# Packed attention with a gated convolution: the low-word pass of the float64 weights and eight scaled query tables move to GpSimd, with a new issue order

## The chip, the core and the metric

The kernel runs on one core of a Trainium2 chip. The metric is the device time of one execution in microseconds. The core has four compute engines with queues of their own: TensorE (PE; its weight loads are listed as PEld), VectorE (DVE), ScalarE (ACT) and GpSimd (POOL). SyncE (SP) issues all transfers here.

## The reference, cut to what matters

```python
def sm_attn(qq, kk, vv):                      # 8 batches, 8 heads, head size 64
    s = scale * np.matmul(qq, kk.transpose(0, 1, 3, 2))
    s = s - np.max(s, axis=-1, keepdims=True)
    a = np.exp(s)
    a = a / (np.sum(a, axis=-1, keepdims=True) + 1e-09)
    return np.matmul(a, vv)
p_packed = sm_attn(p, k, v)                   # 32 packed queries against 576 keys
x = sm_attn(q, p_packed, p_packed)            # 576 queries against the 32 packed rows

h = np.maximum(x @ w_in, 0.0)                 # 512 -> 1024
conv_out = sum over 3 taps of conv_w[k] * h shifted along the sequence
out = (h * sigmoid(conv_out)) @ w_out         # 1024 -> 512, 8 x 576 rows
```

q, k, v and p come as float32. w_in, conv_w and w_out come as float64, so each weight is a pair of 32-bit words and has to be narrowed on the core.

## The kernel before, in words

Sixteen head groups g (four heads of one batch each, two groups to a batch) run through the same steps. `queries(g)` (L481) makes two copies of the packed queries scaled by 1/8, the tile `pm` (ACT, L484), transposes it on PE (L487) and copies the result to `pT`. `head_transpose` (L420) brings keys and queries into the layout that PE needs: for the first four groups by PE transposes (L444) and ACT copies (L450), later by DVE (L427). `attention(g)` (L509) computes scores of keys (L460), a maximum on DVE (`nm`, L515), the exponential on ACT (`a`, L519), transposes `a` on PE (L547), multiplies by v (L557), scales to `pb` (L576), transposes that to `ppT` (L581, L584), computes the scores of the queries (L460 again), and then a softmax of six DVE passes over 128x576 (L591 to L615). The result is split in a high and a low part, `a2hi` (ACT, L619) and `a2lo` (DVE, L621).

`packed_weight(b, hf)` (L632) multiplies the packed rows of batch b with one half of w_in (PE, L641), and splits the sum in `ghi` (ACT, L656) and `glo` (for the first two batches by PE and ACT, L660 and L664). `ffn1(b, j)` (L689) then has eight steps j for a batch. One step, a unit below, is 24 matmuls of L705, a copy out of PSUM (ACT, L717), three DVE passes and two ACT passes. A unit waits for a2 and for glo of its batch. `ffn2` and what follows it (L794 and the products of L926) multiply by w_out.

The weights come as eight tiles of 128x1024 pairs, four of w_in (i = 0 to 3) and four of w_out (i = 4 to 7), into three staging areas: one tile `stage`, and two parts of a tile that the trace shows as `hgt`. `narrow` (L267) makes float32 of a tile in three passes: ACT rescales the upper words in place (L275), DVE turns the low words into a three-bit integer in place (L277), DVE joins the two (L282). The first two need only the landed tile. Tiles 0 and 1 are needed by `packed_weight(0, 0)`, tiles 2 and 3 by `packed_weight(0, 1)`.

The order of the work is written out: `ORDER` is a list of two-digit numbers of streams, `Flow.run` takes the next step of that stream each time, and each engine's queue gets its instructions in that order. `Flow` also estimates when each step can start, from costs written into the steps and from constants. The estimate has one effect on the program: where it sees PE idle before the step "second" (the first L794), `fill` places matmuls of the identity with itself, the tile `idle` (L251), in PE's queue. They compute nothing that is used.

Of the kernel before, what the change touches and what calls it, by code (L numbers as in the profile page):

```python
# [13 lines left out]
ALU = mybir.AluOpType  # L14
# [7 lines left out]
    "0002043m0408043u0304030305060b3l0c06013k050b060c0g0c0c0b060605053q3v3k0e06070e070a3k063v06063k0j060e3v09060j3s0k"  # L22
    "0f0j0o060k0e0f3n0k0i0h3r3r060k0d063k0e0m0d3k3r060d0r0e0e0d060e060e060m060e0m0r3t0m0m3t0s0r400e3w0w0s0e0s0n0z0e0e"
    "3t0s0l0e0n060z0z0l0l0e3y170e46460m0q060m0e0u0e0u0l0m460m0e41460p410m170m0e0m0u17480u3x493x480v410v0m0u3x48410m4a"
    "49484a10474849474a3z0m414948413z491f4a49124248470u0u4a4a474b124b0t490u124b0t14433z0u0t0m4a434b0m4c0t4d1f4b4b434c"
    "0u441f4d0x4c4b3z12120u4e18434e3z1a0u4c120m4d4c4g3o6e130u1a154c3z0u131a124c6e450m0u434e4d45126e0u4e434g4f0m456e4g"
    "1a0u1n0m0u124f6e1n451l4d4e4f6e0u454f4d1a4h1c4e4e0u0u4f4g1b0y1k4d451b4i4f4f114j4i881n884k4i6e1g4h6f4j6e6e4i6f6e4k"
    "4h4k4i4j4i89161i121a4k4j4i6e1i6f6f121e1a4j4k4l891d126f6f6f6f4j4k4l1i6f1o4k6g121s4l1i4l6g4h124l8a4m1a4l6f1a1j4m1q"
    "191j1i1a6f4m4j121i6g1q8a1w6g6h6e4n6g4m6h1q204n1a1v6g1i6g4m1v4l1h6g4m1a4n124m121r1v4n6g6g236f8b1a6g4o121i4n1i4o4p"
    "6h6h4o4p4p1a236h124o8b4o6h4n1q6g4p1a6h6h6h4p6h4o1m4o1a1y4n234p4p1q1i6h1i1q4q282b1y4r6i1r1y6i1y1a1i6i126i6i1q1a2b"  # L30
    "4r6i12241a4q4q1z6i6j1a6i1a4r1i6i6i4s6i2b1p4s6j4s1q4t4u1q4s1i1y1i4t4s264t1t4t1q1z6k1y2g6j2c4u6j1y4u4s261i6j2j4u6j"
    "4s6k6j264u2j4v4t2j1q6j271i4u1u4v226i4u6j266j4t2e1x4w2k6j4t1i4v1q2e1i1q6k4w2e4v2a1i1q6h2f2e4v3p6k6k6k4w1y1i274x26"
    "6k1q6k6l1y4x6l216k6k6k2f4x1q6k4x2m1y4v50266m1q6l6l4w264v1q26262r2m6l2h4w6l2m2r506l4x2r6j6l4y4w2e1q2n2z4y4y2z1y1y"
# [19 lines left out]
class Step:  # L53
# [5 lines left out]
    def __init__(self, engine, ns, after=(), take=(), give=(), sets=None, cols=0, tiled=False, parts=1, loose=False):  # L59
        self.engine, self.ns, self.after, self.take, self.give = engine, ns, after, take, give  # L60
        self.sets, self.cols, self.tiled, self.parts, self.loose = sets, cols, tiled, parts, loose


class Flow:
# [14 lines left out]
        "DVE": dict(PE=256, ACT=128, DVE=127, SP=200, POOL=200),  # L79
        "DATA": dict(PE=300, ACT=300, DVE=300, SP=0, POOL=0),  # L80
    }
    ISSUE = dict(SP=(465, 1100), POOL=(1050, 1000))
    LATER, LANES = 620, 8
    SLOW = ((4600, 1.28), (5500, 1.7))

    def __init__(self, tokens, warm, busy):
        self.tokens = {k: [(0.0, None)] * n for k, n in tokens.items()}
        self.warm, self.busy = warm, busy
        self.done = {}
        self.free = dict(PE=2500.0, ACT=1900.0, DVE=600.0, SP=580.0, POOL=1350.0)  # L90
        self.data = 2700.0
        self.issued = 0
        self.flights = [0.0] * 7
        self.windows = {}
        self.tiled = False
        self.streams = []
# [4 lines left out]
    def earliest(self, step, last):  # L101
# [3 lines left out]
        at = max([t + self.LAG[e][step.engine] if e else 0.0 for t, e in froms], default=0.0)  # L105
        return max(at, self.free[step.engine] + (self.tail(step.tiled) if step.engine == "PE" else 0))
# [36 lines left out]
    def transfers(self, step, at):  # L143
        issue, delay = self.ISSUE[step.engine]
        for _ in range(step.parts):
            if step.engine == "SP":
                at = max(at, self.flights.pop(0))
            at += self.LATER if step.engine == "SP" and self.issued >= self.LANES else issue
            self.issued += step.engine == "SP"
            slow = next((x for t, x in self.SLOW if self.data < t), 1.0)  # L150
            self.data = max(self.data, at + delay) + step.ns / step.parts * slow
            if step.engine == "SP":
                self.flights.append(self.data)
        return at, self.data

    def run(self, order):
        for n in order:
# [12 lines left out]
            elif step.engine in self.ISSUE:  # L170
                self.free[engine], t = self.transfers(step, at)
                end = (t, "DATA")
            else:
                end = (at + step.ns, engine)
                self.free[engine] = end[0]
            for name in step.give:
# [8 lines left out]
def tile_packed_attention_conv_gate(  # L185
# [11 lines left out]
    nc = tc.nc  # L197
# [19 lines left out]
    PE_LO = 2  # L217
    HALVED = 4
# [50 lines left out]
    def narrow(key, out, raw, m, after=(), take=(), sets=None):  # L269
# [30 lines left out]
    def load_weight(i):  # L300
        _, _, src, st = weight_tile(i)
        yield Step("SP", 2500, after=[("wp", i - 3)] if i >= 3 else [], sets=[("wd", i)])
# [80 lines left out]
    def load_v(g):  # L383
        b, gg = divmod(g, NG)
        yield Step("SP", 2250, take=["v"], sets=[("v", g)], parts=2)
# [683 lines left out]
```

## Time and profile before

| what | value |
|---|---|
| median of 3 runs | 402.41 us (402.21 to 402.48) |
| the profiled execution's own time | 402.01 us |
| its span | 400.2 us |
| PE busy | 392.2 us, 98% of the span |
| DVE busy | 365.5 us, 91% |
| ACT busy | 284.1 us, 71% |
| POOL busy | 1.6 us |
| bytes moved | 49.19 MB |

Times of rows are in microseconds from the start of the span. The profiled execution took 1.8 us more than its span. Busy times of PE come from modelled ends, so consecutive matmuls overlap a little in the rows; the distance from one start to the next is the better measure of what one costs.

### The profile page before, as it was taken

To read this page: it belongs to the slowest core of one execution; us is meant where nothing else is said; L and a number is where in the kernel's file an instruction comes from. 1 tells how busy PE (TensorE), PEld (TensorE's weight loads), DVE (VectorE), ACT (ScalarE), POOL (GpSimd) and SP (SyncE) were. 2 spreads that over 40 slices of the span, in tenths; PEclk is the share of its full clock that TensorE was granted. 3 is DMA by queue.
4 is the path that set the end of the run, shared out by engine and by line. 5 is a ranking of instruction groups with operands and counts; after the bars stand their busy time and mean duration, and the time that the engine had idled before them with its cause. 6 is when DMAs were issued, how large, how long until landed. Compare 5 with 4: busy or idle time off the path is not lost.

```text
span 400.2 us, 8463 instructions
## 1 busy us (share of the span) xinstructions
PE 392.2 (98%) x3393; PEld 318.8 (80%) x3393; DVE 365.5 (91%) x532; ACT 284.1 (71%) x497; POOL 1.6 (0%) x16
## 2 busy tenths in 40 slices
PE   7899999999999999999999999999999999999996
PEld 6668676778868877878869687878788787889996
DVE  0789999999999999999999999999999999999751
ACT  4989999977687588666765659738657678876440
POOL 1000000000000000000000000000000000000000
PEclk9999999999999999999999999999999999999999
DMA  8999999999858782966483539113600110001202
GB/s 304 357 361 267 276 264 163 128 156 146 121 94 112 122 196 68 156 88 153 79 153 79 97 100 157 48 51 97 122 2 27 52 41 19 23 2 52 78 28 79
DMA packets 140378, 49.19 MB, mean 123 GB/s; under 512 B 121244, under 2 KB 132788, under 8 KB 140340
## 3 DMA queue, kind: packets, MB, share of 16 engines
q1 hardware_dynamic: 140340, 48.67, 55.8%
q8 instruction: 26, 0.43, 0.5%
q14 instruction: 12, 0.10, 0.1%
HBM read 37.25 MB, written 9.44 MB: 117 GB/s over the span
## 4 chain that ended last, share of the span: by engine, by line
PE 84%; ACT 8%; DMA 5%; SPq 1%; issue 1%
PE fo L794 44%; PE big L705 23%; PE big L460 3%; PE big L641 3%; DMA q<-in_q_dram 3%; PE big L926 3%; DMA v<-in_v_dram 2%; PE sm L926 2%; PE sm L557 2%; ACT hgt L731 1%; ACT hgt L721 1%; PE big L547 1%; ACT hgt L275 1%; ACT glo L664 1%; SPq L404 1%; PE sm L794 1%
## 5 line engine op out<-in xcount | busy, mean ns | idle before, releaser
L794 PE MATMUL fo<-wo_hi,xhi 128*128 128x512 f32 x240 | 97.9, 408 | 0.0
L794 PE MATMUL fo<-wo_lo,xhi 128*128 128x512 f32 x240 | 94.8, 395 | 0.0
L794 PE MATMUL fo<-wo_hi,xlo 128*128 128x512 f32 x240 | 94.5, 394 | 0.0
L717 ACT ACTIVATE hbuf<-big 128x576 f32<-128x576 f32 x64 | 42.3, 668 | 30.1 <-PE big L705 29.5
L731 ACT ACTIVATE hgt<-hgt 128x576 f32<-128x576 f32 x64 | 43.9, 696 | 18.8 <-DVE hgt L727 18.6
L794 PEld LDWEIGHTS fo<-wo_hi,xhi 128*128 128x128 f32 x240 | 45.3, 189 | 13.3 <-issue 2.5
L705 PE MATMUL big<-a2hi,ghi 128*128 128x288 f32 x256 | 55.6, 298 | 0.1
L705 PE MATMUL big<-a2hi,glo 128*128 128x288 f32 x256 | 54.5, 294 | 0.0
L705 PE MATMUL big<-a2lo,ghi 128*128 128x288 f32 x256 | 54.3, 294 | 0.0
L794 PEld LDWEIGHTS fo<-wo_lo,xhi 128*128 128x128 f32 x240 | 45.1, 188 | 11.2
L723 DVE SCALAR_TENSOR_TENSOR hgt<-hbuf,cw,hgt 128x576 f32<-128x576 f32 x64 | 51.1, 802 | 2.5 <-ACT hgt L721 2.3
L794 PEld LDWEIGHTS fo<-wo_hi,xlo 128*128 128x128 f32 x240 | 45.1, 188 | 7.9
L727 DVE SCALAR_TENSOR_TENSOR hgt<-hbuf,cw,hgt 128x576 f32<-128x576 f32 x64 | 50.7, 803 | 0.4
L721 ACT ACTIVATE hgt<-hbuf,cw 128x576 f32<-128x576 f32 x64 | 50.3, 792 | 1.0
L733 DVE SCALAR_TENSOR_TENSOR hgt<-hgt,hbuf 128x576 f32<-128x576 f32 x64 | 47.1, 745 | 0.7 <-ACT hgt L731 0.4
L705 PEld LDWEIGHTS big<-a2hi,ghi 128*128 128x128 f32 x256 | 42.7, 188 | 5.1 <-ACT glo L664 1.0
L705 PEld LDWEIGHTS big<-a2lo,ghi 128*128 128x128 f32 x256 | 40.9, 188 | 0.0
L705 PEld LDWEIGHTS big<-a2hi,glo 128*128 128x128 f32 x256 | 40.9, 188 | 0.0
L747 DVE TENSOR_TENSOR xlo<-hgt,xhi 128x1024 fp32r<-128x1024 f32 (+1 forms) x36 | 35.8, 1002 | 0.0
L858 ACT COPY o<-fo 128x512 f32<-128x512 f32 (+1 forms) x32 | 18.5, 580 | 21.2 <-PE fo L794 19.6
L744 ACT CAST xhi<-hgt 128x1024 fp32r<-128x1024 f32 (+1 forms) x36 | 31.5, 881 | 2.2 <-DVE hgt L733 2.2
L515 DVE TENSOR_REDUCE nm<-big 128x1 f32<-128x576 f32 x16 | 11.9, 746 | 11.6 <-PE big L460 11.5
(191 smaller groups left out, 604.1 us busy)
## 6 DMA issues: line engine op xcount, KB each, us to landing
out_dram<-o SPq DMA_DIRECT2D x35, 256.0 KB, 3.3
v<-in_v_dram SPq DMA_DIRECT2D x16, 512.0 KB, 5.9
k<-in_k_dram SPq DMA_DIRECT2D x48, 144.0 KB, 4.2
q<-in_q_dram SPq DMA_DIRECT2D x48, 144.0 KB, 4.1
hgt<-in_moe_w_in_dram SPq DMA_DIRECT2D x3, 1024.0 KB, 11.2
hgt<-in_moe_w_out_dram SPq DMA_DIRECT2D x3, 1024.0 KB, 6.6
a1T<-stage SPq DMA_DIRECT2D x96, 20.0 KB, 1.8
hgt<-in_k_dram SPq DMA_DIRECT2D x2, 576.0 KB, 5.1
```

Of the source, the lines that this page charges most:

```text
L705: nc.tensor.matmul(out=t[:, hf, :SH], lhsT=w[:, gg, js], rhs=x[:, hf * SH : (hf + 1) * SH], start=n == 0, stop=n == 3 * NG - 1,)
L717: nc.scalar.activation(out=h[:, 1 : S + 1].rearrange("c (f s) -> c f s", f=2), in_=t[:, :, :SH], func=AF.Relu, scale=0.5)
L721: nc.scalar.activation(out=d, in_=h[:, 1 : S + 1], func=AF.Copy, scale=cw[:, NJ + j : NJ + j + 1])
L723: nc.vector.scalar_tensor_tensor(out=d, in0=h[:, 0:S], scalar=cw[:, j : j + 1], in1=d, op0=ALU.mult, op1=ALU.add)
L727: nc.vector.scalar_tensor_tensor(out=d, in0=h[:, 2 : S + 2], scalar=cw[:, 2 * NJ + j : 2 * NJ + j + 1], in1=d, op0=ALU.mult, op1=ALU.add)
L731: nc.scalar.activation(out=d, in_=d, func=AF.Tanh)
L733: nc.vector.scalar_tensor_tensor(out=d, in0=d, scalar=1.0, in1=h[:, 1 : S + 1], op0=ALU.add, op1=ALU.mult)
L744: nc.scalar.copy(out=hi[:, js, o], in_=src[:, js])
L747: nc.vector.tensor_tensor(out=lo[:, js, o], in0=src[:, js], in1=hi[:, js, o].bitcast(F32), op=ALU.subtract)
L794: nc.tensor.matmul(out=t[:, : fs.stop - fs.start], lhsT=x, rhs=w[:, c, fs], start=c + i == 0, stop=c == NJ - 1 and i == 2)
L858: nc.scalar.copy(out=o[:, fs], in_=sums_of[m, q][:, : fs.stop - fs.start])
L926: nc.tensor.matmul(out=turns[m, bank][:, at : at + 256], lhsT=x[:, c, :], rhs=y[:, c, :], start=first and c + i == 0, stop=c == 3 and i == ...
```

## The change

The lines of the new file that matter, without the new list of numbers (two of its lines stand for it) and without the marks `cols=1` that nine more DVE steps got:

```diff
-    "0002043m0408043u0304030305060b3l0c06013k050b060c0g0c0c0b060605053q3v3k0e06070e070a3k063v06063k0j060e3v09060j3s0k"
+    "000404040402053l3m080303030505060106050b0b3k0b060j3u070c0c0c0j0j060c0e3k07060e3k060606063k0r060e063v0g3k3k0k0k0a"
...
+        "POOL": dict(PE=300, ACT=300, DVE=300, SP=300, POOL=150),
...
-    ISSUE = dict(SP=(465, 1100), POOL=(1050, 1000))
-    LATER, LANES = 620, 8
+    ISSUE = dict(SP=(465, 1100), POOL=(900, 1000))
+    LATER, LANES = 640, 8
...
+    ROOMY, SLACK = 60000, 500
+    RING = 288
...
+        if step.engine in ("DVE", "POOL") and step.cols:
+            at = max(at, self.port)
...
+                while self.queued and (self.queued[0][0] <= at or sum(n for _, n in self.queued) + step.ring > self.RING):
+                    at = max(at, self.queued.pop(0)[0])
...
+    SCALED = 8
+    BY_POOL = range(8)
+    POOL_LOW, POOL_BOTH = 1500, 2200
...
-        yield Step("DVE", 68 + m * 100 // 192, after=after, loose=True)
-        nc.vector.tensor_scalar(
+        pool = key in BY_POOL
+        side = nc.gpsimd if pool else nc.vector
+        at = Step("POOL", POOL_LOW, after=after, loose=True, parts=0, sets=[("low", key)], cols=1)
+        yield at if pool else Step("DVE", 68 + m * 100 // 192, after=after, loose=True, cols=1)
+        side.tensor_scalar(
             out=low.bitcast(I32), in0=low.bitcast(U32), scalar1=2.0**-29, scalar2=7.0, op0=ALU.mult, op1=ALU.min
         )
-        yield Step("DVE", 69 + m * 100 // 96, after=[("up", key)], take=take, sets=sets)
+        yield Step("DVE", 69 + m * 100 // 96, after=[("up", key)] + [("low", key)] * pool, take=take, sets=sets, cols=1)
...
-        yield Step("ACT", 200, after=[("p", g // 4)] + [("pT", g - 1)] * (g > 0), take=["pm"])
+        pool = g < SCALED
+        after = [("p", g // 4)] + [("pT", g - 1)] * (g > 0)
+        yield Step("POOL", 400, after=after, take=["pm"], parts=0, cols=1) if pool else Step("ACT", 200, after=after, take=["pm"])
...
-        nc.scalar.mul(out=pm, in_=packs[g // 4][:, g % 4, :].unsqueeze(1).broadcast_to([128, 2, D]), mul=SCALE)
+        twice = packs[g // 4][:, g % 4, :].unsqueeze(1).broadcast_to([128, 2, D])
+        if pool:
+            nc.gpsimd.tensor_scalar(out=pm, in0=twice, scalar1=SCALE, scalar2=None, op0=ALU.mult)
+        else:
+            nc.scalar.mul(out=pm, in_=twice, mul=SCALE)
```

So the low-word passes of all eight weight tiles leave DVE for POOL, the small one of conv_w stays on DVE, and `pm` of groups 0 to 7 leaves ACT for POOL. In `Flow`, DVE steps that carry the mark `cols=1` and POOL's steps never overlap; transfers are held back by a limit of queued work, `RING`; and after 60 us a transfer counts as landed 0.5 us later. `Flow` itself runs on no engine: what is left of it in the program is the order and the fillers.

The order moves three places of which the prediction speaks. The new file's lines are 23 to 29 higher. The first is SP's queue, where the first weights are loaded (`stage` and `hgt_77` are staging areas; `hgt_76` holds the first keys and queries). Before:

```order
L349 DMA s_158<-in_moe_conv_w_dram 24x256
L404 DMA k<-in_k_dram 128x1152
L305 DMA hgt_77<-in_moe_w_in_dram 128x2x1024
L404 DMA hgt_76<-in_q_dram 128x1152
L388 DMA v<-in_v_dram 128x4x256
L392 DMA v<-in_v_dram 64x4x64
L305 DMA hgt_77<-in_moe_w_in_dram 128x2x1024
L404 DMA k<-in_k_dram 128x1152
L477 DMA p<-in_p_dram 128x4x64
L404 DMA q<-in_q_dram 128x1152
```

The same place now:

```order
L372 DMA s_156<-in_moe_conv_w_dram 24x256
L328 DMA stage<-in_moe_w_in_dram 128x2x1024
L427 DMA k<-in_k_dram 128x1152
L427 DMA hgt_76<-in_q_dram 128x1152
L328 DMA hgt_77<-in_moe_w_in_dram 128x2x1024
L411 DMA v<-in_v_dram 128x4x256
L415 DMA v<-in_v_dram 64x4x64
L328 DMA hgt_77<-in_moe_w_in_dram 128x2x1024
L427 DMA k<-in_k_dram 128x1152
L427 DMA q<-in_q_dram 128x1152
```

The queries of group 1 (`hgt_76`) now come ahead of weight tile 1, tile 0 (`stage`) behind the first v and conv_w, and the queries of group 2 (`q`) ahead of the second load of p.

The second is ACT's queue from `ghi` of the first packed weight to the copy-out of the first unit. Before:

```order
L656 CAST ghi<-big 128x1024
L576 ACTIVATE pb<-sm,rs 128x128
L450 COPY qT<-big 128x512
L584 COPY ppT<-sm 128x128
L619 CAST a2hi<-a2t 128x576
L275 ACTIVATE stage<-stage 128x1024
L664 CAST glo<-big 128x1024
L519 ACTIVATE a_564,sm_565<-big,nm 128x576
L493 COPY pT<-sm 128x2x32 x2
L275 ACTIVATE hgt_77<-hgt_77 128x1024
L717 ACTIVATE hbuf_78<-big 128x576
```

The same place now:

```order
L685 CAST ghi<-big 128x1024
L295 ACTIVATE stage<-stage 128x1024
L548 ACTIVATE a_494,sm_495<-big,nm 128x576
L473 COPY qT<-big 128x512
L605 ACTIVATE pb<-sm,rs 128x128
L648 CAST a2hi<-a2t 128x576
L613 COPY ppT<-sm 128x128
L693 CAST glo<-big 128x1024
L356 CAST wo_hi<-tmp 128x1024
L295 ACTIVATE hgt_77<-hgt_77 128x1024
L524 COPY pT<-sm 128x128
L746 ACTIVATE hbuf_78<-big 128x576
```

The exponential of group 3 stands ahead of `glo` now, and `wo_hi` ahead of the first copy-out.

The third is POOL's queue after its work of setting up. Before:

```order
L246 MEMSET v 64x4x64
masks.py:199 ISA
masks.py:199 AFFINE_SELECT ident<-ident 128x128
L246 MEMSET v 64x4x64
L527 MEMSET stage 128x2x32 x2
```

The same place now:

```order
L511 TENSOR_SCALAR pm<-p 128x128 x4
L300 TENSOR_SCALAR stage<-stage 128x1024
L300 TENSOR_SCALAR hgt_77<-hgt_77 128x1024 x2
L300 TENSOR_SCALAR stage<-stage 128x1024
L511 TENSOR_SCALAR pm<-p 128x128
L300 TENSOR_SCALAR hgt_77<-hgt_77 128x1024
L511 TENSOR_SCALAR pm<-p 128x128
L300 TENSOR_SCALAR hgt_77<-hgt_77 128x1024
L511 TENSOR_SCALAR pm<-p 128x128
L300 TENSOR_SCALAR hgt_77<-hgt_77 128x1024 x2
L511 TENSOR_SCALAR pm<-p 128x128
L556 MEMSET stage 128x2x32 x2
```

Sixteen instructions were added there: four tables, tiles 0, 1, 2 and 4, and then tables and tiles by turns, so that a tile can stand behind a table that has to wait.

On PE the order holds 35 filler calls before and 33 now; 31 stand ahead of the first unit in both, 4 behind it before, 2 now.

## Rows read from the trace of the kernel before

**Rows 1.** The page: share of the span and instructions of PE.
```profile
PE 392.2 (98%) x3393; PEld 318.8 (80%) x3393; DVE 365.5 (91%) x532; ACT 284.1 (71%) x497; POOL 1.6 (0%) x16
```

**Rows 2.** Windows: length; busy PE, PEld, DVE, ACT, POOL (instructions); PEclk, DMA share, GB/s.
```profile
16.00:24.00 8.00, 6.41 (x95) 5.13 (x95) 7.25 (x13) 5.61 (x13) 0.00 (x0) 1.00 1.06 362
32.00:40.00 8.00, 8.00 (x73) 7.18 (x74) 7.83 (x13) 8.00 (x15) 0.24 (x2) 1.00 1.01 232
...
80.00:140.00 60.00, 60.00 (x614) 47.90 (x614) 59.50 (x90) 42.83 (x82) 0.00 (x0) 1.00 0.86 125
```

**Rows 3.** The tile idle (fillers): ns min/median/max, first and last start.
```profile
L251 PE MATMUL idle<-ident x70: 271/275/579, 1.7 to 48.3; 128*128 128x128 f32 x70
```

**Rows 4.** PE's timeline: start, busy, line, operation, [idle before it].
```profile
17.59 0.83 PE L251 MATMUL idle<-ident 128*128 128x128 f32 x6
19.95 0.74 PE L444 MATMUL big<-ident,hgt 128*128 128x128 f32 x5 [1.52 <-DMA hgt<-in_q_dram]
...
33.45 1.73 PE L251 MATMUL idle<-ident 128*128 128x128 f32 x14
34.93 0.51 PE L705 MATMUL big<-a2hi,ghi 128*128 128x288 f32 x2
...
45.09 0.83 PE L251 MATMUL idle<-ident 128*128 128x128 f32 x6
45.85 0.77 PE L557 MATMUL sm<-v,a1T 128*32 128x64 f32 x40
...
48.23 0.38 PE L251 MATMUL idle<-ident 128*128 128x128 f32 x2
48.85 0.77 PE L444 MATMUL big<-ident,q 128*128 128x128 f32 x5 [0.24 <-ACT glo L664]
```

**Rows 5.** The chain of waits in order of time: start, length, what.
```profile
15.99 12.05 DMA q<-in_q_dram
```

**Rows 6.** PE's timeline at two more places.
```profile
28.18 0.74 PE L444 MATMUL big<-ident,q 128*128 128x128 f32 x5 [0.54 <-DMA q<-in_q_dram]
28.75 0.27 PE L487 MATMUL sm<-ident,pm 128*128 128x128 f32 x1
...
29.39 1.09 PE L641 MATMUL big<-w_in_sb,ppT 64*32 64x512 f32 x16
...
36.61 0.74 PE L547 MATMUL big<-ident,a 128*128 128x128 f32 x5
37.11 0.51 PE L705 MATMUL big<-a2hi,ghi 128*128 128x288 f32 x2
```

**Rows 7.** ACT's timeline around glo.
```profile
30.59 1.01 ACT L656 CAST ghi<-big 128x1024 fp32r<-128x1024 f32 x1 [0.37 <-PE big L641]
...
34.07 1.02 ACT L664 CAST glo<-big 128x1024 fp32r<-128x1024 f32 x1
34.96 0.78 ACT L519 ACTIVATE a<-big,nm 128x576 f32<-128x576 f32 x1
35.69 0.36 ACT L493 COPY pT<-sm 128x64 f32<-128x64 f32 x2
```

**Rows 8.** Groups of instructions: shapes, count | busy us, mean ns | idle before.
```profile
L484 ACT ACTIVATE pm<-p 128x128 f32<-128x128 f32 x16 | 5.3, 332 | 0.2 <-DMA p<-in_p_dram 0.2
L275 ACT ACTIVATE hgt<-hgt 128x1024 f32<-128x1024 f32 x6 | 7.4, 1237 | 0.0
L277 DVE TENSOR_SCALAR hgt<-hgt 128x1024 int32<-128x1024 uint32 x6 | 4.1, 687 | 0.9 <-DMA hgt<-in_moe_w_in_dram 0.8
```

**Rows 9.** POOL's timeline.
```profile
1.07 0.30 POOL L246 MEMSET v<- 64x256 f32 x1
1.41 0.29 POOL masks.py:199 TENSOR_SCALAR_AFFINE_SELECT ident<-ident 128x128 f32<-128x128 f32 x1
...
37.45 0.24 POOL L527 MEMSET stage<- 128x64 f32 x2 [35.50 <-DVE tmp L282]
```

**Rows 10.** DVE's timeline beside POOL's last instruction.
```profile
37.34 0.73 DVE L597 TENSOR_TENSOR s<-s,mx 128x576 f32<-128x576 f32 x1
```

More of the change, by code (lines that the diff above doesn't have):

```diff
@@ L90, in __init__ @@
         self.free = dict(PE=2500.0, ACT=1900.0, DVE=600.0, SP=580.0, POOL=1350.0)
[L91 removed]
+        self.data = dict(SP=2700.0, POOL=2700.0)
         self.issued = 0
         self.flights = [0.0] * 7
+        self.queued = []
+        self.port = 0.0
         self.windows = {}
@@ L147, in transfers @@
                 at = max(at, self.flights.pop(0))
+                while self.queued and (self.queued[0][0] <= at or sum(n for _, n in self.queued) + step.ring > self.RING):
+                    at = max(at, self.queued.pop(0)[0])
             at += self.LATER if step.engine == "SP" and self.issued >= self.LANES else issue
             self.issued += step.engine == "SP"
-            slow = next((x for t, x in self.SLOW if self.data < t), 1.0)
-            self.data = max(self.data, at + delay) + step.ns / step.parts * slow
+            slow = next((x for t, x in self.SLOW if self.data["SP"] < t), 1.0)
+            ns = step.ns / step.parts * slow
+            start = max(self.data[step.engine], at + delay)
             if step.engine == "SP":
-                self.flights.append(self.data)
-        return at, self.data
+                landed = self.data["SP"] = start + ns
+                self.flights.append(landed)
+                self.queued.append((landed, step.ring))
+            else:
+                landed = self.data["POOL"] = start + min(max(0.0, self.data["SP"] - start), ns) + ns
+                self.data["SP"] = max(self.data["SP"], start) + ns
+        return at, landed + (self.SLACK if at > self.ROOMY else 0.0)
     def run(self, order):
@@ L175, in run @@
                 self.free[engine] = end[0]
+                if engine != "ACT" and step.cols:
+                    self.port = end[0]
             for name in step.give:
@@ L301, in load_weight @@
         _, _, src, st = weight_tile(i)
-        yield Step("SP", 2500, after=[("wp", i - 3)] if i >= 3 else [], sets=[("wd", i)])
+        yield Step("SP", 2500, after=[("wp", i - 3)] if i >= 3 else [], sets=[("wd", i)], ring=16)
         if src.dtype != F32:
@@ L595, in attention @@
         nc.vector.tensor_reduce(out=mx, in_=s3, axis=AX.X, op=ALU.max)
-        yield Step("DVE", 669)
+        yield Step("DVE", 669, cols=1)
         nc.vector.tensor_tensor(
@@ L608, in attention @@
         nc.vector.reciprocal(out=sm, in_=sm)
-        yield Step("DVE", 669)
+        yield Step("DVE", 669, cols=1)
         nc.vector.tensor_tensor(
@@ L725, in ffn1 @@
         )
-        yield Step("DVE", 729)
+        yield Step("DVE", 729, cols=1)
         nc.vector.scalar_tensor_tensor(
@@ L744, in convert @@
             nc.scalar.copy(out=hi[:, js, o], in_=src[:, js])
-        yield Step("DVE", 68 + (js.stop - js.start) * 128 * 100 // 96, sets=spans)
+        yield Step("DVE", 68 + (js.stop - js.start) * 128 * 100 // 96, sets=spans, cols=1)
         for src, o in cuts:
```

75 lines of the change are left out of this document (38 added, 37 removed).

## The prediction

> **What bounds the kernel now.** I read the page first: PE is busy for 392.2 of 400.2 us [rows 1]. Then the windows: from 80 to 140 us PE shows 60.00 of 60 us, with DVE at 59.50 and ACT at 42.83 [rows 2], so there PE is the limit and DVE keeps up, barely. What PE loses lies ahead of that. The list by tile shows 70 filler matmuls, the last at 48.3 us [rows 3], and PE's timeline shows after each stretch of fillers how much longer PE waited: from 17.59 to 19.95 for a load, from 33.45 to 34.93, from 45.09 to 45.85, from 48.23 to 48.85 [rows 4]. The reader should see that fillers are lost time that looks busy, and that behind 48.85 there are none. The amount of real matmul work is the same in both programs, so **the time changes by what is lost ahead of the last filler, and by nothing else unless a new stall appears later**. A filler call costs 0.21 us: 14 records, two to a call, from 33.45 to 34.93 [rows 4].
>
> Last, what ends that loss. The chain of waits runs through the load of the queries of group 2, issued at 15.99 and on the way for 12.05 us [rows 5]; PE takes it up at 28.18 and only then comes to the first packed weight at 29.39 [rows 6]. From 32 to 40 us ACT is busy all the time [rows 2], and the chain is in ACT's queue: `ghi` at 30.59, `glo` at 34.07 [rows 7], the first unit at 34.93 [rows 4]. So the opening is first a matter of loads, then of ACT.
>
> **The change part by part.**
>
> Tables of the queries: 8 instructions of 332 ns leave ACT [rows 8], 2.7 us of busy time. The first ones stood where ACT has idle time (5.61 of 8 us busy from 16 to 24 [rows 2]), and one stood just ahead of `ghi`, which waited for PE anyway, 0.37 us [rows 7]. I cost this at nothing by itself: the cover is ACT's idle time and that wait; were the cover gone, only the few tables between `ghi` and the last filler would count, up to 0.7 us.
>
> Low-word passes: 8 passes of 687 ns leave DVE [rows 8], 5.5 us of busy time. From 32 to 40 us DVE is busy for 7.83 of 8 [rows 2], but the first unit was released by ACT's `glo`, so I cost it at nothing too; the cover is ACT. If ACT got shorter, DVE would be next.
>
> The same work on POOL: the trace has no such pass there. From one side, a memset of 256 elements in a row took 0.30 us, which makes 1.2 us for 1024 elements; from the other, AFFINE_SELECT over 128 took 0.29, which makes 2.3 us [rows 9]. I take 1.5, nearer to the memset, because these spans hold a fixed part that does not grow with the elements. Does it lie on the path? ACT's pass over the upper words takes 1.24 us [rows 8], needs the same landed tile, and stands in a queue that is full. So POOL's pass is done no more than about one microsecond after ACT's even at 2.3, and the joining pass on DVE comes later in DVE's queue in any case. Zero, with an upper bound of one late tile, 1.1 us; a gain is excluded, since the pass is slower in any case. Each table costs POOL 0.15 to 0.3 us by the same rows, in place of 0.33 on ACT. A tile behind a table waits for what the table waits for (the table before it must have been copied to `pT`); this concerns tile 3 and later ones, whose readers come after the first units.
>
> Loads: the queries of group 1 pass ahead of a weight tile of 1024 KB. At 362 GB/s [rows 2] that is 2.9 us, which would do away with the wait up to 19.95 [rows 4]. But PE then waits for the queries of group 2, and ahead of those only the 128 KB of p have gone: 0.36 us. The gain is between 0.36 and 2.4 (the stretch from 17.59 to 19.95, if the later load didn't bind). I take 0.4, because the chain has the later load in it [rows 5]. The first weight tile comes one v later, some 590 KB or 1.6 us, and still many microseconds ahead of 29.39.
>
> From there to the packed weight: before 1.21 us, five transposes (0.57), one of a table and four more [rows 6]. Now five transposes and two filler calls: 0.57 + 0.43 = 1.00. Minus 0.2.
>
> From `ghi` to `glo`: 3.48 us before [rows 7]. Between them ACT had `pb`, `qT`, `ppT`, `a2hi` and a weight tile; now it has the same and the exponential, 34.96 to 35.69 with its read-out [rows 7], that stood behind `glo` before. Plus 0.73. So the first unit starts at 34.93 - 0.4 - 0.2 + 0.7 = 35.0, much as before. But more work is done by then: one more transposed `a`, 36.61 to 37.11 [rows 6], one table less, 0.11 [rows 6]. Minus 0.39.
>
> Behind the first unit: 4 filler calls before, in stretches that lost 0.76 and 0.62 [rows 4], 1.38 us for 0.85 of fillers. Now 2 calls, 0.43; in the same proportion 0.70. Between 0.43 (no wait beyond the fillers) and 1.38 (as much as before); I take 0.70, since all of PE's stretches above end later than their fillers. Minus 0.68.
>
> Sum: -0.4 - 0.2 + 0.73 - 0.39 - 0.68 = -0.94 us. 402.01 of the profiled execution becomes 401.1; that execution stands 0.4 under the median shown, so the median goes from 402.41 to 401.5.
>
> Here a page speaks against the change. What the trace shows of POOL beside DVE is one memset pair at 37.45 [rows 9], during which a DVE pass with two inputs took 0.73 us [rows 10]; POOL did not read there. The Trainium skill (SBUF — State Buffer, "Who interferes with whom") says that a DVE instruction with two SBUF inputs and a GpSimd instruction that reads SBUF lock each other out for a whole instruction. No run here shows it yet. By that rule the sum would be that of the third rival below.
>
> **The rivals.**
>
> *The opening stays bound by loads alone.* For it: DMA is at its full share from 16 to 40 us (1.06, 1.01 [rows 2]). Then what PE saves comes back as a wait for the next load; only the last term survives, -0.68, and the exponential ahead of `glo` costs its 0.73: 402.4. Against it: the loads ahead of `ghi` are no more than before.
>
> *The loads were the whole misfit.* If the new order of loads does away with the two waits for queries (1.52 and 0.54 [rows 4, 6]) and the rest goes as in my sum without its own load term: -2.1 - 0.5 = -2.6, 399.8. For it: both are waits for a load that now has less ahead of it. Against it: the load that binds last has gained only 128 KB.
>
> *POOL holds DVE up.* Five or six low-word passes fall ahead of the last filler, four of them where DVE is full. If each keeps DVE from its next two-input pass for 1.5 us, and 0.6 us less work is there in return, DVE loses 0.9 us four times, 3.6 us, and `a2lo`, the joining passes and the convolution's passes come late. DVE has 0.2 us of idle time in 8 [rows 2]; 0.6 over the three windows from 24 to 48, which leaves 3.0, and the units then wait for DVE instead of ACT: 402.4 - 0.9 + 3.0 = 404.5. It decides from the point where a pass on POOL takes longer than DVE's saving and its slack, some 0.8 us a time, and falls on two-input passes. For it: the joining pass, the softmax's subtraction, `a2lo` and the convolution's passes all have two inputs. Against it: while POOL reads, DVE can do transposes and reductions, and the new marks in `Flow` keep such steps apart in its estimate, for a pass of 1.5 us.
>
> *The change doesn't do what it says.* If POOL's tables came so late that `pT` waits, ACT's gain would be a wait; that would show as the first rival, and has its chance in it.
>
> **How the numbers follow.** What a measurement can tell from no change is about 0.2%, 0.8 us. My forecast, 0.45: 400.6 to 402.0, most of it just beyond 0.2%. Loads alone, 0.25: 402.0 to 402.8. The whole misfit, 0.13: near 399.8. POOL against DVE, 0.17: 403.3 to 405. Faster: 0.13 and 0.37 of the 0.45, together 0.50. Same: 0.08 of the forecast, the 0.25, and a little of the last, 0.34. Slower: 0.16. The range reaches from 399.5, the second rival with its bounds, to 403.8, into the third; it leaves out some 0.15.
>
> **What would show it.** Right: the first L734 (the units' new line) starts near 35 us, the last filler ends near 44 (35.0, three units of 24 matmuls, a tile of w_out and a packed weight later) with no more than 0.3 us of wait behind it, PE is at 60.00 of 60 us from 80 on, and DVE's busy time falls by about 5 us, ACT's by 2.7. The wait for `hgt` from in_q is gone from the PE's list, the one for `q` is still there. POOL's low-word pass lies between 1.2 and 2.3 us. Wrong: DVE's two-input passes get longer or wait beside POOL's rows (third rival); fillers or waits behind 49 us; `stage` or `hgt` on POOL last before a joining pass that PE waits for; or a first unit that starts before 33.5 (second rival).

## The result, and the profile after

The changed kernel takes **405.14 us** (median of 4 runs, 404.59 to 405.65); the kernel before takes 402.45 (median of 4, 402.21 to 403.31). The ratio is **1.0062, with a 95% interval from 1.0043 to 1.0080**: slower by more than the 0.2% that the prediction took as the least that can be told. The forecast was 401.5 in a range from 399.5 to 403.8, so the time lies outside the range and on the other side. The profiled execution took 405.3 us, its span is 403.5, which is 3.3 longer than before.

The page of the kernel after, its busy row (as [rows 1]) and the group of the new POOL passes:

```profile
PE 392.5 (97%) x3389; PEld 318.1 (79%) x3389; DVE 365.0 (90%) x524; ACT 282.6 (70%) x489; POOL 40.8 (10%) x32
...
L300 POOL TENSOR_SCALAR hgt<-hgt 128x1024 int32<-128x1024 uint32 x6 | 24.7, 4118 | 15.0 <-DVE hgt L752 7.2
```

A low-word pass takes 4.1 us on POOL, six times the 0.687 that it took on DVE [rows 8] and far outside the bounds of 1.2 to 2.3. And DVE, which gave up 5.5 us of work, is busy for 365.0 us, 0.5 less than before. PE is as busy as before; the span is what grew.

The windows of after (columns as in [rows 2]):

```profile
32.00:40.00 8.00, 7.94 (x103) 6.71 (x102) 6.75 (x12) 8.00 (x15) 7.84 (x3) 1.00 0.84 220
40.00:48.00 8.00, 6.10 (x49) 3.55 (x55) 7.55 (x10) 6.55 (x12) 6.48 (x4) 1.00 1.09 232
80.00:140.00 60.00, 60.00 (x605) 47.42 (x611) 58.94 (x89) 44.70 (x89) 0.00 (x0) 1.00 0.69 138
```

From 80 to 140 us PE is at 60.00 of 60, as before: the loss lies in the opening. From 32 to 40 POOL is full, and DVE is busy for 6.75 us where it had 7.83. From 40 to 48 PE shows 6.10 of 8.

POOL's timeline of after (start, length, engine, line, operation, [idle before it]):

```profile
9.23 0.53 POOL L511 TENSOR_SCALAR pm<-p 128x128 f32<-128x128 f32 x1 [0.81 <-PE sm L516]
12.99 3.84 POOL L300 TENSOR_SCALAR stage<-stage 128x1024 int32<-128x1024 uint32 x1 [3.23 <-DMA stage<-in_moe_w_in_dram]
20.25 3.80 POOL L300 TENSOR_SCALAR hgt<-hgt 128x1024 int32<-128x1024 uint32 x1 [3.42 <-DMA hgt<-in_moe_w_in_dram]
24.53 4.45 POOL L300 TENSOR_SCALAR hgt<-hgt 128x1024 int32<-128x1024 uint32 x1 [0.47 <-DMA hgt<-in_moe_w_in_dram]
30.40 4.25 POOL L300 TENSOR_SCALAR stage<-stage 128x1024 int32<-128x1024 uint32 x1 [1.42 <-DVE w_in_sb L305]
34.73 1.57 POOL L511 TENSOR_SCALAR pm<-p 128x128 f32<-128x128 f32 x1
36.38 3.96 POOL L300 TENSOR_SCALAR hgt<-hgt 128x1024 int32<-128x1024 uint32 x1
40.42 1.57 POOL L511 TENSOR_SCALAR pm<-p 128x128 f32<-128x128 f32 x1
42.08 3.86 POOL L300 TENSOR_SCALAR hgt<-hgt 128x1024 int32<-128x1024 uint32 x1
```

From 24.53 to 46 us POOL is a queue without a gap but one. Passes and tables stand in each other's way: a table that takes 0.53 us alone (9.23) takes 1.57 where it starts together with a joining pass on DVE, and the pass behind it starts that much later.

DVE's timeline of after, the operations that the sections below speak of:

```profile
13.40 0.78 DVE L300 TENSOR_SCALAR s<-s 24x128 int32<-24x128 uint32 x1
...
20.35 1.06 DVE L635 TENSOR_SCALAR sm<-sm 128x18 f32<-128x18 f32 x1
...
21.86 0.76 DVE L639 TENSOR_TENSOR s<-s,sm 128x576 f32<-128x576 f32 x1
...
29.02 1.24 DVE L305 SCALAR_TENSOR_TENSOR w_in_sb<-hgt 128x1024 int32<-128x1024 int32 x1 [1.43 <-POOL hgt L300]
...
34.69 1.24 DVE L305 SCALAR_TENSOR_TENSOR tmp<-stage 128x1024 int32<-128x1024 int32 x1 [0.18 <-POOL stage L300]
...
40.38 1.23 DVE L305 SCALAR_TENSOR_TENSOR w_in_sb<-hgt 128x1024 int32<-128x1024 int32 x1 [1.31 <-POOL hgt L300]
...
42.18 1.63 DVE L752 SCALAR_TENSOR_TENSOR hgt<-hbuf,cw,hgt 128x576 f32<-128x576 f32 x1
43.85 0.82 DVE L756 SCALAR_TENSOR_TENSOR hgt<-hbuf,cw,hgt 128x576 f32<-128x576 f32 x1
44.59 0.17 DVE L635 TENSOR_SCALAR sm<-sm 128x18 f32<-128x18 f32 x1
44.66 0.81 DVE L752 SCALAR_TENSOR_TENSOR hgt<-hbuf,cw,hgt 128x576 f32<-128x576 f32 x1
```

Two things are to be seen. First **waits**: joining passes (L305) stand in DVE's queue until POOL is done, 1.43 and 1.31 us, with 0.67 at 24.09 and 0.18 at 34.69 some 3.6 us in all. Second **holds**: operations that wait for no semaphore get longer. L635 takes 0.17 us elsewhere and 1.06 here, L752 0.81 elsewhere and 1.63 here; both start 0.1 us after a POOL pass. There are three operations ahead of 49 us that are longer by over half a microsecond, 2.3 us in all (the third is the small L300 at 13.40, which took 0.22 in the kernel before), and five ahead of 75, 4.1 us. These 4.1 us are most of the 5.0 by which DVE's busy time failed to fall.

PE's timeline of after (as [rows 4, 6]):

```profile
30.32 0.63 PE L670 MATMUL big<-w_in_sb,ppT 64*32 64x512 f32 x4 [0.77 <-DVE w_in_sb L305]
...
36.77 0.53 PE L734 MATMUL big<-a2hi,ghi 128*128 128x288 f32 x2
...
42.05 0.33 PE L516 MATMUL sm<-ident,pm 128*128 128x128 f32 x1 [0.23 <-POOL pm L511]
...
45.51 0.71 PE L271 MATMUL idle<-ident 128*128 128x128 f32 x4
47.88 0.72 PE L483 MATMUL big<-kT,pT 64*32 64x288 f32 x16 [1.66 <-DVE kT L450]
```

The first packed weight waits half way for the joining pass of a weight tile. The first unit starts at 36.77 (34.93 before). And behind the last filler PE waits for `kT`, a DVE step: from 45.51 to 47.88 nothing useful happens. ACT's `ghi` and `glo` (as [rows 7]):

```profile
31.45 1.01 ACT L685 CAST ghi<-big 128x1024 fp32r<-128x1024 f32 x1 [2.07 <-PE big L670]
...
35.70 1.02 ACT L693 CAST glo<-big 128x1024 fp32r<-128x1024 f32 x1
```

The chain of waits of after (start, length, what) has POOL in it twice, with the pass of tile 1, between its load and its joining pass, and with that of tile 3, which stands behind a table in POOL's queue:

```profile
10.75 13.71 DMA hgt<-in_moe_w_in_dram
...
24.53 4.46 POOL hgt L300
...
29.02 1.25 DVE w_in_sb L305
...
36.38 3.97 POOL hgt L300
```

**A correction.** The section on the change and the prediction count the first weight tiles wrongly. They are loaded in the order 2, 0, 1: the one in `stage`, called tile 0 there, is tile 2, and the one that the queries of group 1 pass, called tile 1, is tile 0. The third to land, at 24.5 us, is tile 1, and the first packed weight needs it. In the kernel before tile 1's two DVE passes stood here:

```profile
24.19 0.69 DVE L277 TENSOR_SCALAR hgt<-hgt 128x1024 int32<-128x1024 uint32 x1 [0.81 <-DMA hgt<-in_moe_w_in_dram]
...
27.35 1.22 DVE L282 SCALAR_TENSOR_TENSOR w_in_sb<-hgt 128x1024 int32<-128x1024 int32 x1
```

The joining pass ended at 28.57, 0.8 us ahead of the packed weight at 29.39 [rows 6]. Two smaller points: the second tile in `stage` is tile 5, not 4, and a unit has 12 matmuls, not 24 (the page of after has 256 of each of three kinds for 64 units).

### The profile page after: what moved, and what is told of

Read it like the earlier page. It is cut to its first block, busy times and chain, and to the rows that moved or that the text cites. A ratio compares the mean times of both kernels' runs of the same rounds, so it can differ in the third digit from the quotient of the medians.

```text
span 403.5 us, 8471 instructions
## 1 busy us (share of the span) xinstructions
PE 392.5 (97%) x3389; PEld 318.1 (79%) x3389; DVE 365.0 (90%) x524; ACT 282.6 (70%) x489; POOL 40.8 (10%) x32
## 4 chain that ended last, share of the span: by engine, by line
PE 84%; DMA 5%; DVE 4%; POOL 2%; ACT 2%; issue 1%; SPq 1%; DVEq 0%; ACTq 0%
PE fo L823 44%; PE big L734 22%; DMA hgt<-in_moe_w_in_dram 3%; PE big L483 3%; PE big L670 3%; PE big L955 3%; PE sm L955 2%; POOL hgt L300 2%; PE sm L586 2%; DMA v<-in_v_dram 2%; DVE hgt L756 1%; DVE hgt L752 1%; PE big L576 1%; PE sm L823 1%; PE big L361 1%
## 5 line engine op out<-in xcount | busy, mean ns | idle before, releaser
L823 PE MATMUL fo<-wo_hi,xhi 128*128 128x512 f32 (+1 forms) x240 | 97.1, 405 | 0.0
L823 PE MATMUL fo<-wo_lo,xhi 128*128 128x512 f32 (+1 forms) x240 | 94.4, 393 | 0.0
L823 PE MATMUL fo<-wo_hi,xlo 128*128 128x512 f32 (+1 forms) x240 | 94.2, 392 | 0.0
L752 DVE SCALAR_TENSOR_TENSOR hgt<-hbuf,cw,hgt 128x576 f32<-128x576 f32 x64 | 52.2, 819 | 3.8 <-ACT hgt L750 3.7
L756 DVE SCALAR_TENSOR_TENSOR hgt<-hbuf,cw,hgt 128x576 f32<-128x576 f32 x64 | 52.4, 823 | 0.6
L300 POOL TENSOR_SCALAR hgt<-hgt 128x1024 int32<-128x1024 uint32 x6 | 24.7, 4118 | 15.0 <-DVE hgt L752 7.2
```

Of the source, the lines that this page charges most:

```text
L300: side.tensor_scalar(out=low.bitcast(I32), in0=low.bitcast(U32), scalar1=2.0**-29, scalar2=7.0, op0=ALU.mult, op1=ALU.min)
L752: nc.vector.scalar_tensor_tensor(out=d, in0=h[:, 0:S], scalar=cw[:, j : j + 1], in1=d, op0=ALU.mult, op1=ALU.add)
L756: nc.vector.scalar_tensor_tensor(out=d, in0=h[:, 2 : S + 2], scalar=cw[:, 2 * NJ + j : 2 * NJ + j + 1], in1=d, op0=ALU.mult, op1=ALU.add)
L823: nc.tensor.matmul(out=t[:, : fs.stop - fs.start], lhsT=x, rhs=w[:, c, fs], start=c + i == 0, stop=c == NJ - 1 and i == 2)
```

## The experiments

**The theory** after this reading: a pass of 4 us on POOL makes joining passes late, those of tiles 1 and 3 above all, and PE waits for them or for what is queued behind them on DVE. **The rivals**: the new order costs the time, whoever does the passes; or the tables do; or what POOL reads holds DVE up, and the waits add little. Twelve kernels were run, each compared with the kernel before on the same chip; order_only, low_on_dve, pm_on_act and old_order_pool were run on one chip, beside_only, the two with tiles on DVE and half_pool on a second, the other four on a third, so ratios of different groups stand against different executions of the kernel before. "Low" is who does the low-word passes, "tables" who makes the eight scaled tables. The two times are of PE, from each kernel's one profiled execution: when the first unit starts, and when PE goes on behind the last filler (in the new order that is a product with `kT`, in the old order a transpose of `q`). Executions of one kernel differ too: on the third chip the kernel before took 401.8 to 405.0 us in 35 of them. So a few tenths between two rows of these columns say little, and old_order_half's profiled execution was the slowest of its 12.

| kernel | order | low | tables | ratio to before, 95% | first unit | PE goes on | span |
|---|---|---|---|---|---|---|---|
| before | old | DVE | ACT | 1 | 34.93 | 48.85 | 400.2 |
| after | new | POOL | POOL | 1.0062 (1.0043 to 1.0080) | 36.77 | 47.88 | 403.5 |
| order_only | new | DVE | ACT | 1.0006 (0.9994 to 1.0018) | 35.86 | 45.99 | 401.2 |
| low_on_dve | new | DVE | POOL | 0.9987 (0.9971 to 1.0004) | 35.56 | 45.80 | 400.7 |
| pm_on_act | new | POOL | ACT | 1.0039 (1.0024 to 1.0054) | 36.85 | 47.35 | 402.3 |
| old_order_pool | old | POOL | POOL | 1.0047 (1.0031 to 1.0064) | 36.05 | 50.61 | 401.9 |
| old_order_pm_pool | old | DVE | POOL | 0.9991 (0.9974 to 1.0007) | 35.29 | 49.00 | 400.3 |
| beside_only | new | DVE, POOL reads for nothing | ACT | 1.0114 (1.0096 to 1.0132) | 38.03 | 48.64 | 405.0 |
| tile1_dve | new | POOL, tile 1 DVE | POOL | 1.0065 (1.0041 to 1.0088) | 35.85 | 47.28 | 402.9 |
| tiles13_dve | new | POOL, tiles 1 and 3 DVE | POOL | 1.0000 (0.9987 to 1.0014) | 36.38 | 46.45 | 401.0 |
| half_pool | new | half each | POOL | **0.9958 (0.9942 to 0.9973)** | 34.57 | 44.41 | 399.5 |
| quarter_pool | new | a quarter POOL | POOL | 0.9977 (0.9966 to 0.9988) | 35.19 | 45.19 | 399.9 |
| half_pm_act | new | half each | ACT | 1.0018 (1.0007 to 1.0029) | 35.69 | 46.19 | 401.6 |
| old_order_half | old | half each | POOL | 1.0009 (0.9993 to 1.0025) | 35.41 | 50.92 | 402.2 |

In the new order the span less the time at which PE goes on is between 354.5 and 355.6 us, but for beside_only (356.4); in the old order it is 351.3 each time. So the column "PE goes on" is where a kernel of this order is won or lost.

### Which part of the change costs: four kernels

order_only puts both pieces of work back and keeps the order and the fillers; the next two put back one piece each (one of the two lines below).

```diff
-        side = nc.gpsimd if pool else nc.vector
+        side = nc.gpsimd if False else nc.vector
...
-        if pool:
+        if False:
             nc.gpsimd.tensor_scalar(out=pm, in0=twice, ...
```

> The new order and its fillers, with the low-word passes on DVE and the query tables on ACT, as before. Theory A (DVE's joining passes and PE wait for POOL's low-word passes, which took 3.8 to 4.5 us each): most of the 2.7 us lost comes back and the order alone gives 401 to 402.5 us. Theory B (the new order loses by itself, by its loads and by the exponential ahead of glo): 404 us or more. Theory C (the tables on POOL are what costs): 402.5 or less, as in A; the next two runs tell A from C.

> The changed kernel with only the low-word passes back on DVE; the eight tables stay on POOL, fillers as in the changed kernel. A: 401 to 402.5, within 0.6 of the run with both undone; the first unit starts 1.5 us or more earlier than at 36.77. B: 404 or more. C: 404 or more, since the tables are still on POOL.

> The changed kernel with only the eight tables back on ACT; the low-word passes stay on POOL. A: 404.3 to 405.5, the first unit still near 36.8 and the wait behind the last fillers near 47.9 still there. B: 404 or more. C: 401 to 402.8.

Of the medians, low_on_dve's 402.32 lies in the range of theory A; order_only's 403.15 lies above A's and below B's, and pm_on_act's 404.24 just below A's. The first unit of low_on_dve is 1.2 us earlier than in after, not 1.5 or more.

The order alone is neutral (1.0006). With the tables on POOL it becomes 0.9987, with the low words on POOL 1.0039, with both 1.0062. So the low words cost 0.33% where ACT makes the tables and 0.75% where POOL makes them too. A reason that the rows suggest is the shared queue: without tables (pm_on_act) the pass of tile 3 starts at 35.33 instead of 36.38, and its joining pass doesn't wait. It is held instead by the next POOL pass, 2.15 us long where 1.23 is usual; no run separates the two. DVE's timeline of pm_on_act:

```profile
39.74 2.15 DVE L305 SCALAR_TENSOR_TENSOR w_in_sb<-hgt 128x1024 int32<-128x1024 int32 x1
```

In order_only no DVE operation is stretched and none waits for POOL. PE's timeline of order_only:

```profile
35.86 0.53 PE L734 MATMUL big<-a2hi,ghi 128*128 128x288 f32 x2
...
44.16 0.71 PE L271 MATMUL idle<-ident 128*128 128x128 f32 x4
45.99 0.72 PE L483 MATMUL big<-kT,pT 64*32 64x288 f32 x16 [1.12 <-DVE kT L450]
```

The kernel after is 0.91 us later at the first unit, another 0.98 later from there to `kT`, and waits 0.46 more at 66.47: 2.35 us, and the spans differ by 2.3.

The old order with both pieces on POOL, by the same two edits made in the kernel before:

> The order and the fillers of the kernel before, with the low-word passes and the eight tables on POOL. A: slower than before by more than the change itself, 405 to 409, because in the old order the joining pass stands nearer behind the landing of its tile (tile 1 joined at 27.35, 3.2 us after its low-word pass began) and DVE waits there 1 to 2 us at each of the first tiles. B: 402 to 403.5, since the old order is kept.

The ratio is 1.0047 and the median 404.40 us, slower than theory B's range and under theory A's: the cost of POOL does not come from the new order, and it is no greater in the old one, where A had it greater.

### Do holds alone cost anything: beside_only

DVE keeps its passes and ACT its tables. Behind each low-word pass POOL reads the identity twice with the same operation, 512 elements each time, into an area that nobody uses. No compute engine waits for it.

```diff
+        if pool:
+            scrap = spare[:, 4 * DFF : 4 * DFF + 512]
+            nc.gpsimd.tensor_copy(out=scrap[:, :1], in_=low[:, :1])
...
+            for _ in range(2):
+                nc.gpsimd.tensor_scalar(
+                    out=scrap.rearrange("r (a c) -> r a c", a=8).bitcast(I32),
+                    in0=pairs.bitcast(U32), scalar1=2.0**-29, scalar2=7.0, op0=ALU.mult, op1=ALU.min)
```

> The new order with the low-word passes on DVE and the tables on ACT (as in the run of the order alone, 1.0006 of before), and beside them as much reading work on POOL that nobody waits for: behind each low-word pass POOL copies one element of it and then makes two passes of 512 elements from the identity into unused space. Theory A (DVE and PE wait for the results of POOL's long passes): no more than 0.1% over the order alone, 0.9995 to 1.0020. Theory D (POOL's reading holds up DVE's passes with two inputs, 0.8 us at each start in the changed kernel's trace): 1.0030 to 1.0050, as with the passes really on POOL (1.0039 with tables on ACT).

The ratio is 1.0114, against 1.0006 for order_only. No step of PE, ACT or DVE waits for POOL here, so work beside DVE costs by itself. DVE's timeline of beside_only, three operations; in order_only L300 takes 0.63 to 0.70 us and the pass that makes `a2lo` (L650 there) 0.75:

```profile
26.40 1.18 DVE L300 TENSOR_SCALAR hgt<-hgt 128x1024 int32<-128x1024 uint32 x1
...
30.99 1.23 DVE L663 TENSOR_TENSOR a2lo<-a2t,a2hi 128x576 fp32r<-128x576 f32 x1
...
37.94 1.15 DVE L300 TENSOR_SCALAR hgt<-hgt 128x1024 int32<-128x1024 uint32 x1
```

One of the kinds held has two inputs, the other has one. The stretches add up to 2.84 us ahead of 49 and 4.01 ahead of 75. This is no exact copy of the change: POOL works on each tile in two passes of 2.0 to 3.0 us, and DVE has its own low-word passes besides. It shows that holds can cost by themselves as much as the whole change did, not how much of the change's own loss they are. The range that was expected by waits alone missed, and the one by holds, 1.0030 to 1.0050, was too low.

### Do the waits cost: tile1_dve and tiles13_dve

```diff
-        side = nc.gpsimd if pool else nc.vector
+        side = nc.gpsimd if pool and key != 1 else nc.vector
```

> The changed kernel (1.0062 of before) with the low-word pass of weight tile 1 alone on DVE, seven on POOL. A: tile 1's joining pass starts near 28 instead of 29.0, the first unit about 0.9 us earlier than at 36.77, ratio 1.0035 to 1.0050. D: one hold of eight less, 1.0055 to 1.0062. If the tables are what matters most: 1.005 or more too.

> The same with the low-word passes of tiles 1 and 3 on DVE, six on POOL. A: the wait of DVE for tile 3 (1.31 us at 40.38) goes too, and PE's wait behind the last fillers shrinks from 1.66 to 1.1 us; ratio 1.0010 to 1.0030. D: 1.0045 to 1.0060, since six of eight holds remain.

tile1_dve takes away the wait at 29.02, and the first unit starts at 35.85, the same as in order_only; but the time stays at 1.0065. That is more than theory A's range; within its interval it fits theory D's range or the tables' as well. The gain was lost again further on, as DVE's and PE's timelines of tile1_dve show:

```profile
39.79 1.23 DVE L305 SCALAR_TENSOR_TENSOR w_in_sb<-hgt 128x1024 int32<-128x1024 int32 x1 [1.38 <-POOL hgt L300]
```

```profile
41.46 0.33 PE L516 MATMUL sm<-ident,pm 128*128 128x128 f32 x1 [0.59 <-POOL pm L511]
...
47.28 0.72 PE L483 MATMUL big<-kT,pT 64*32 64x288 f32 x16 [1.65 <-DVE kT L450]
```

From the first unit to `kT` it takes 11.43 us (11.11 in after, 10.13 in order_only). With tile 3 on DVE as well (tiles13_dve) that stretch is 10.07, and the time is 1.0000, outside theory D's range and a little better than A's. PE's timeline of tiles13_dve:

```profile
36.38 0.50 PE L734 MATMUL big<-a2hi,ghi 128*128 128x288 f32 x2
...
46.45 0.72 PE L483 MATMUL big<-kT,pT 64*32 64x288 f32 x16 [0.71 <-DVE kT L450]
```

So the long passes of these two tiles together carry 0.6% of the cost, and taking away the first alone leaves the wait at the second. The first unit of tiles13_dve is hardly earlier than in after, so nearly all of its gain lies behind it; tile 3 alone on DVE was not run, and how much of the 0.6% needs tile 1 is not shown.

### A shorter pass: half_pool, quarter_pool

Each low-word pass is cut by columns: POOL does 512 of 1024 (or 256), DVE the rest.

```diff
+        cut = m // 2 if pool else 0
+        for eng, part in ((nc.gpsimd, low[:, :cut]), (nc.vector, low[:, cut:])):
+            if part.shape[1]:
+                eng.tensor_scalar(out=part.bitcast(I32), in0=part.bitcast(U32), ...
```

> The changed kernel with each low-word pass cut in two: POOL does 512 elements, DVE the other 512. If POOL's time goes by the element (128 elements of a table took 0.53 us, 1024 took 3.84), its pass takes 1.9 to 2.1 us; if a fixed part or the number formats make it long, 3 us or more. A: with passes half as long tile 1's joining pass waits for nothing of POOL and the ratio falls to 1.000 to 1.003. D: the holds are as many as before, 1.004 to 1.006.

> The same with POOL doing 256 of the 1024 low words of each tile, DVE 768, tables on POOL. Theory A (what counts is that no pass is waited for, and DVE's time): POOL's pass about 1.1 us, no DVE wait, and DVE saves half as much: between the halved kernel and the one with all passes on DVE, 0.9960 to 0.9985. Theory D (holds scale with POOL's reading): holds halve again, which gives back 0.2 us of the 0.5 us before 49 us: 0.9950 to 0.9970.

half_pool is **faster than both kernels: 0.9958**, below every range that was expected (its median is 401.55 us, that of the kernel before beside it 402.83). POOL's and DVE's timelines of half_pool around tile 1, and PE's:

```profile
24.08 2.29 POOL L303 TENSOR_SCALAR hgt<-hgt 128x512 int32<-128x512 uint32 x1 [2.55 <-DMA hgt<-in_moe_w_in_dram]
```

```profile
24.03 0.45 DVE L303 TENSOR_SCALAR hgt<-hgt 128x512 int32<-128x512 uint32 x1
...
26.65 1.22 DVE L308 SCALAR_TENSOR_TENSOR w_in_sb<-hgt 128x1024 int32<-128x1024 int32 x1
```

```profile
34.57 0.53 PE L737 MATMUL big<-a2hi,ghi 128*128 128x288 f32 x2
...
42.86 0.71 PE L271 MATMUL idle<-ident 128*128 128x128 f32 x4
44.41 0.72 PE L486 MATMUL big<-kT,pT 64*32 64x288 f32 x16 [0.84 <-ACT wo_lo L368]
```

POOL's half ends at 26.37, 0.28 us before DVE's queue comes to the joining pass, and nowhere does DVE wait for POOL. The stretches fall from 2.3 us to about 0.5 ahead of 49. What PE waits for behind the last filler is now an ACT step. With a quarter the pass takes 1.1 to 1.9 us and the stretches are about 0.5 again, while DVE has more of its own work left: 0.9977, in theory A's range.

### Does half_pool need the rest of the change: half_pm_act, old_order_half, old_order_pm_pool

half_pm_act is half_pool with the tables back on ACT; the other two are the kernel before with halves and tables on POOL, and with the tables alone.

> The kernel with halved low-word passes (0.9958 of before) with the eight tables back on ACT. If the tables on POOL are part of the gain, as the pair order alone (1.0006) and tables on POOL (0.9987) suggests: 0.997 to 0.999. If the halved passes are all of it: 0.9950 to 0.9965.

> The order and fillers of the kernel before with halved low-word passes and the tables on POOL. If the new order is needed for the gain: 0.999 to 1.003. If the new order is neutral, as the run of the order alone says (1.0006): 0.995 to 0.998.

> The kernel before with nothing but the eight tables moved to POOL. From my prediction's step (tables cost nothing, ACT has idle time early): 0.999 to 1.001. From the pair of runs in the new order (1.0006 to 0.9987): 0.997 to 0.999.

With ACT's tables the halves give 1.0018, outside both ranges that were expected, so beside them the tables on POOL are worth 0.6%. PE's and ACT's timelines of half_pm_act show two places, POOL's and DVE's a third:

```profile
7.60 0.33 PE L519 MATMUL sm<-ident,pm 128*128 128x128 f32 x1 [0.52 <-ACT pm L516]
```

```profile
32.72 0.32 ACT L516 ACTIVATE pm<-p 128x128 f32<-128x128 f32 x1
```

```profile
24.47 2.10 POOL L303 TENSOR_SCALAR hgt<-hgt 128x512 int32<-128x512 uint32 x1 [2.41 <-DMA hgt<-in_moe_w_in_dram]
```

```profile
24.59 0.89 DVE L303 TENSOR_SCALAR hgt<-hgt 128x512 int32<-128x512 uint32 x1
```

PE waits for ACT's tables three times ahead of 12 us (0.52, 0.56 and 0.37), and one table stands between `ghi` and `glo` again, which are 4.55 us apart, against 4.27 in half_pool. The third place: DVE's half of tile 1 starts 0.12 us behind POOL's and is held to 0.89 us, where in half_pool it starts 0.05 us ahead of it and takes 0.45. Such stretches are 2.0 us ahead of 49 in half_pm_act, with the same passes on POOL. How the 0.6% splits between the three places is not shown. In the old order tables on POOL alone can't be told from no change (0.9991), and neither can halves and tables together (1.0009), both as the first range of each had it: without the new order no gain shows.

## Why the prediction was wrong, point by point

- **The step that failed: "I take 1.5" for POOL's pass, between 1.2 and 2.3.** The trace had no such pass, and the bounds came from a memset and an AFFINE_SELECT [rows 9], neither of which is a pass of two operations from one type to another. Measured: 3.80 to 4.45 us; a table took 0.53, not 0.15 to 0.3. With half the elements and 2.0 us (half_pool) DVE waits for POOL nowhere, as the reasoning had it for 1.5.
- **The wait that was put at nothing: "the joining pass on DVE comes later in DVE's queue in any case. Zero".** This fell with the size, and with the mix-up of tiles. Tile 1 lands at 24.5, its joining pass had 0.8 us to spare, and DVE stood still in front of it: 1.43 us there, and `ghi` was 1.45 us late (31.45, where the prediction's terms put it at 30.0). The stated upper bound of "one late tile, 1.1 us" was too small, and there were two late tiles, one behind the other; tiles13_dve shows that together they carry 0.6%.
- **"Behind the first unit", 0.70.** From the last filler's start to PE's going on it is 2.37 us in after, and 1.83 even in order_only. The proportion of idle time to fillers said nothing about what ends the stretch: a transpose of keys on DVE (`kT`), which no row of the prediction looked at.
- **The gain of order and tables, -0.94 us with the passes at nothing:** nearest to it is low_on_dve, 0.9987, which is -0.5 us with an interval from -1.2 to +0.2, so it is neither shown nor excluded. Its parts were off: the first unit starts there at 35.56, not 35.0, and PE goes on at 45.80, where the last filler was to end near 44. The wait for the queries of group 1 is gone, and so is that for group 2, which was to stay; but PE now waits for a load of v (in after 1.11 us at 21.86). And "I cost this at nothing by itself", said of the tables, did not hold in the new order: with ACT's tables PE waits for them three times ahead of 12 us, and beside half passes they are worth 0.6%.
- **The signs named beforehand:** three of the signs of "wrong" are in the rows above: two-input passes that get longer or wait, a joining pass behind POOL that PE waits for, and a wait behind 49 us (0.46 at 66.47). Of the signs of "right" POOL's pass is outside 1.2 to 2.3 us, DVE's busy time is not 5 us lower, the wait behind the last filler is 1.66, not 0.3, and ACT's busy time fell by 1.5 us, not 2.7.
- **Right:** from `ghi` to `glo` 4.25 us (3.48 + 0.73 = 4.21 predicted); PE is at 60.00 of 60 us from 80 to 140, and behind 49 us little is lost (0.46 and 0.17); the time is decided ahead of the last filler.
- **The rivals.** The third, "POOL holds DVE up", gave 404.5 and a chance of 0.17; the time is 405.14. Its point of decision, a pass longer than DVE's saving and slack together, some 0.8 us, was passed by far. (Its 0.6 us of idle time in three windows was one window's 0.2 taken three times; the three have 0.59, 0.17 and 0.03, which would make its time 404.3.) That its number came near is in part luck: it took passes of 1.5 us that hold DVE for their whole length, and the passes take 4 us, hold DVE for 0.9 and are waited for besides. What it had as one price comes in two: late joining passes, and held operations. How the loss splits between them stays open. tiles13_dve takes away most of the waits and leaves 2.1 of the 2.3 us of stretches ahead of 49 (2.1 of 4.1 ahead of 75), and gets 0.6% back; beside_only has holds alone and loses 1.1% against order_only. The two may overlap, since a held operation makes the next ones late only where DVE's queue is full; no run tests that. The first rival, 402.4, is near the order alone (1.0006 is 402.65), though no run tests its reason; the second, 399.8, wanted a first unit before 33.5, and the earliest of any run is 34.57.
- **What spoke against the change.** In these traces POOL is held for the whole of a DVE operation: the tables at 34.73 and 40.42, which started within 0.04 us of a joining pass, end 0.37 and 0.38 us behind its end. The other way round a pass of 3.8 us holds one DVE operation for about 0.9 us (up to 0.5 with 512 elements, 0.2 with 256), and L639 at 21.86 runs at its usual 0.76 within the pass from 20.25 to 24.05. The Trainium skill (SBUF — State Buffer, "Who interferes with whom") says that the one that comes first keeps the other out for its whole instruction; the traces agree for POOL behind DVE and do not for DVE behind POOL. The direction of its warning was right, and the chance of 0.17 was, in hindsight, low.

## What to carry to other kernels

An engine that looks idle isn't free: price the moved pass by a row of the same operation on that engine, and if there is none, allow for a pass several times longer (here six times) and ask which reader has the least time to spare; here tile 1's had 0.8 us. Where the pass can be cut, give the slow engine only as much as it finishes before the reader's queue arrives. And when one late step is mended and the time stays, look for the same step one round later before giving up the theory. Where two engines hold each other up, a tenth of a microsecond in who starts first can decide which of them pays (half_pool and half_pm_act at 24 us).

## What the runs showed of the hardware that was not expected

POOL's time for the two-operation pass grows with its elements: 1.1 us for 256, 2.0 for 512, 3.8 for 1024 where nothing is in its way, about 3.5 ns an element and 0.2 us besides; DVE takes 0.37 to 0.45 us for 512 where POOL does not hold it. A scaled table of 128 elements in float32 takes 0.53 us. DVE operations with one tensor input, L635 with 18 elements in a row and L300 with 1024, were held by POOL as the ones with two inputs were. One hold is shorter where POOL's pass is: up to 1.0 us with 1024 elements, up to 0.5 with 512, some 0.2 with 256. How many there are doesn't follow from the length of the passes: with 512 elements they add up to about 0.5 us ahead of 49 in half_pool and to 2.0 in half_pm_act.
